# Attention with MoE on one core: order-only edges that put a unit's first steps on q behind a sum of the unit two before it

## Chip, core and metric

The kernel runs on one core of a Trainium2 chip. The metric is the device time of one execution in microseconds, the median of the runs. Engines: PE is TensorE, ACT ScalarE, DVE VectorE, POOL GpSimd; SP issues the DMAs.

## The reference

Attention with a causal mask and a memory term for 4 batches, 8 heads, 576 tokens and 64 features a head; its output, 2304 tokens by 512, goes through a two-matrix MLP with a squared ReLU.

```python
def _attn_ref(q, k, v, M_prev, z_prev, beta):
    scores = scale * np.matmul(q, k.transpose(0, 1, 3, 2))
    scores = np.where(causal, -1000000000.0, scores)
    a = np.exp(scores - scores.max(-1, keepdims=True))
    a /= a.sum(-1, keepdims=True) + 1e-09
    local = np.matmul(a, v)
    q_p = np.where(q > 0, q, np.exp(q) - 1.0) + 1.0
    mem_ret = np.einsum('bhsd,bhde->bhse', q_p, M_prev)
    mem_norm = np.einsum('bhsd,bhd->bhs', q_p, z_prev)[..., None] + 1e-06
    g = 1.0 / (1.0 + np.exp(-beta))[None, :, None, None]
    return g * (mem_ret / mem_norm) + (1 - g) * local

def _moe_ref(x, w_in, w_out):
    r = np.maximum(x @ w_in, 0.0)
    return (r * r) @ w_out
```

## The kernel before

The work is cut into 24 **units**. A unit is one batch, one pair of heads, and a list of query tiles of 128 tokens. Batches 0 and 1 (`SEG` is 2) have eight units each: the four head pairs with tiles 1 and 2, and then the four with tiles 3 and 4. Units 0 to 7 are batch 0, 8 to 15 batch 1. Batches 2 and 3 have four units each, with all four tiles (16 to 23). The first 64 tokens of every batch are handled ahead by `first_tokens`.

`attention` is a generator that writes down one unit. Its fore part: a cast of q to `qh` (ACT, L465) and the remainder `ql` (L466), the same for k (L471, L472), then phi(q): `Exp` of q into `pe` (ACT, L482), a ReLU (L487) and L488, then a scale for v (L504 to L521) and the memory term, products `pm` with the memory matrix (PE, L541) and a division. Units 0 to 5 have no casts: they multiply in full float32. The fore part ends with `after()`, which writes down the loads of the next units (`kd`, `qm`, `vv`; q stands in `qm`).

Then the rows of the unit, tile by tile in the order 2, 1, 3, 4: scores on PE (L577) into the one tile `sp`; on DVE the masked scores `e` and their extreme `mx` (L598); on ACT the exponential with its row sums in `sm` (L618; four `sm` buffers); the split of `e` into two halves `a` (ACT L656, DVE L658); a DMA transpose to `aT` (SP, L662); products with v into `acc` (PE, L682); and the sums that add `acc` to the features `feat` (DVE, L685, one for each head). The fore part of unit i+1 is written ahead of the rows of unit i.

When four units have finished a pair of tiles of their batch, their tokens form a block for the MoE (`moe`): `token_halves` scales `feat` into halves `hl` and transposes them to `xT`, and then follow `up` products (PE, L966 to L968), ReLU, square and `gh` (ACT, L972 to L975), `gl` (DVE) and the products `oacc` (PE, L937 to L939). Blocks 1 to 6 run as such; the last two blocks together in `moe_last`. Block 1 is batch 0, tiles 1 and 2 (units 0 to 3), block 2 its tiles 3 and 4 (units 4 to 7). The weights are converted by ACT and DVE in the first 120 us.

What stands where in each engine's queue is decided by a list scheduler when the program is built: it follows the order of writing as priority, its own costs, and edges. An edge of the class `NoSync` (`AFTER`) binds this scheduler alone: no semaphore comes of it, so the chip doesn't wait for the named instruction. An engine runs its queue in order.

Of the kernel before, what the change touches and what calls it, by code (L numbers as in the profile page):

```python
# [14 lines left out]
AF = mybir.ActivationFunctionType  # L15
# [52 lines left out]
SEG = 2  # L68
# [15 lines left out]
AFTER = mybir.DependencyInfo(mybir.DependencyClass.NoSync, mybir.DependencyReason.DATA)  # L84
# [15 lines left out]
def fused_kernel(ctx: ExitStack, tc: tile.TileContext, t0_d, kk_d, qv_d, beta, w_in, w_out, out):  # L100
    nc = tc.nc
# [329 lines left out]
    def loads(i):  # L431
# [13 lines left out]
        nc.sync.dma_start(vv[:, :nv], qv_d[b, p, :, SQ + 2 * ZW : SQ + 2 * ZW + nv])  # L445
        return kd, qm, vv

    def attention(b, p, tiles, ld, after, early, sfull, full, ap, ap_early):
        q_eng, k_eng = (nc.gpsimd if c == 'p' else nc.vector for c in (EARLY if early else LATE))
        late = 0 if early else 1  # L450
        h0 = 2 * p
        tl = tiles[-1]
        kn, ncn = sum(QT[tl]), tl + 1
        qa, qb = QT[tiles[0]][0] - D, kn - D
        kd, qm, vv = ld
        q_raw = qm[:, 2 * ZW :]
# [5 lines left out]
        if not sfull:  # L462
            qh, ql = (ap.tile([P, SQ], F32R, tag=t, name=t) for t in ("qh", "ql"))
            kh, kl = (ap.tile([P, S], F32R, tag=t, name=t) for t in ("kh", "kl"))
            nc.scalar.copy(qh[:, qa:qb], q_raw[:, qa:qb])  # L465
            low = q_eng.tensor_tensor(  # L466
                out=ql[:, qa:qb], in0=q_raw[:, qa:qb], in1=qh[:, qa:qb].bitcast(F32), op=ALU.subtract
            )
            parts.append(low)
            yield  # L470
            nc.scalar.copy(kh[:, :kn], kd[:, :kn])  # L471
            low = k_eng.tensor_tensor(out=kl[:, :kn], in0=kd[:, :kn], in1=kh[:, :kn].bitcast(F32), op=ALU.subtract)  # L472
            parts.append(low)
            yield
            terms = [(qh, kh), (ql, kh), (qh, kl)]
        else:
            terms = [(q_raw, kd)]

        pe = ap.tile([P, 2, S], F32, tag="e", name="pe", bufs=EB if ap is at else EB2)[:, 0]
        w = slice(qa, qb)  # L480
        lead = (b, p, tiles) == order[0]
        ex = nc.scalar.activation(pe[:, w], q_raw[:, w], AF.Exp)  # L482
        if lead:
            later("s", ex)
        ph = pe if sfull else q_raw
# [123 lines left out]
        for i in [t for t in TORD if t in tiles]:  # L609
# [6 lines left out]
            for h in range(2):  # L616
                bs = mx[:n, h, ns - 1 : ns]
                ex = nc.scalar.activation(  # L618
                    e[:n, h, :ke], e[:n, h, :ke], AF.Exp, bias=bs, scale=-1.0, accum_out=sm[:n, h : h + 1]
                )  # L620
# [61 lines left out]
                    nc.tensor.matmul(acc[:n, h], lhs[:, :n], rhs, start=x == 0, stop=x == len(mms) - 1)  # L682
            for h in range(2):
                xo = memx[:n, i - 1, h]
                nc.vector.scalar_tensor_tensor(  # L685
                    out=xo, in0=acc[:n, h], scalar=sm[:n, h : h + 1], in1=xo, op0=ALU.mult, op1=ALU.add
                )
            yield

    def runs(xs):  # L690
# [338 lines left out]
    order = []  # L1029
# [8 lines left out]
    def unit(i):  # L1038
        ld = nxt.pop(0)

        def after():
            while i + len(nxt) + 1 < min(len(order), i + (3 if i + 2 >= AHEAD else 2)):
                nxt.append(loads(i + len(nxt) + 1))

        ap = more[-1] if i > FIRST and i % 2 else at
        early = i < NEF and max(order[i][2]) < 4
        return attention(*order[i], ld, after, i < NEARLY, i < NES, early, ap, i >= WA)
# [87 lines left out]
```

## Time and profile before

| | us |
|---|---|
| three runs: median (lowest to highest) | 585.41 (581.78 to 586.48) |
| the profiled execution, its own time | 584.56 |
| its span, first to last instruction | 582.8 |
| PE, DVE, ACT busy | 527.8, 452.9, 413.1 |

The span is what the rows of the profile cover; the time of an execution has 1.8 us around it. Busy time of PE is that of its matmuls, whose ends are modelled and which overlap: how dense they are is read from their starts.

### The profile page before, as it was taken

Reading aid. Unit: us, or ns where it says so; the run is one execution under the profiler, and the core shown is the slowest. Engines: PE = TensorE matmul, PEld = TensorE weight load, DVE = VectorE, ACT = ScalarE, POOL = GpSimd, SP = SyncE. Lnnn points to the kernel's source line nnn. Section 1 sums busy time; section 2 is a strip of 40 time slices with the busy share of each in tenths; the row PEclk is TensorE's granted clock in tenths of the full one; section 3 lists DMA queues with packets and bytes.
Section 4 is the critical chain, followed back from the end, with each engine's and each line's share of the span. In section 5 each row is a group of like instructions: output and inputs, shape, how many; then the busy total and the mean of one; then the engine's idle time right before and its main releaser. Section 6 shows DMA issues by size and latency. Waiting matters only on the chain.

```text
span 582.8 us, 12609 instructions
## 1 busy us (share of the span) xinstructions
PE 527.8 (91%) x4767; PEld 370.4 (64%) x4767; DVE 452.9 (78%) x1421; ACT 413.1 (71%) x884; POOL 14.9 (3%) x20
## 2 busy tenths in 40 slices
PE   4668988989899988898999999999999999999997
PEld 3546765646576666566777767656677666447766
DVE  6898779798987767989888868696777587744745
ACT  3797997796877776977977768788677643557352
POOL 1010000100110000000000000000000000000000
PEclk9767987999899999999999989999999999999999
DMA  8943971578586556688485394626734440000002
GB/s 317 405 122 74 363 267 37 107 166 179 118 172 127 143 116 124 141 172 178 133 159 138 79 169 87 105 51 132 110 58 86 89 61 2 37 0 2 1 1 72
DMA packets 133132, 71.37 MB, mean 122 GB/s; under 512 B 115408, under 2 KB 121552, under 8 KB 133072
## 3 DMA queue, kind: packets, MB, share of 16 engines
q1 hardware_dynamic: 133072, 70.57, 52.2%
q8 instruction: 37, 0.61, 0.4%
q14 instruction: 23, 0.19, 0.1%
HBM read 37.53 MB, written 4.72 MB: 72 GB/s over the span
## 4 chain that ended last, share of the span: by engine, by line
PE 34%; DVE 31%; ACT 15%; DMA 13%; issue 5%; SPq 1%; POOL 0%; ACTq 0%; DVEq 0%
DVE e L598 5%; DVE a L658 5%; PE seven L834 4%; ACT e L618 4%; DMA aT<-a 3%; DMA qm<-in_qv_dram 3%; PE oacc L939 3%; PE oacc L937 3%; PE oacc L938 3%; PE up L967 3%; PE up L966 3%; PE up L968 3%; PE acc L682 3%; DMA raw<-in_w_in_dram 3%; PE seven L807 2%
## 5 line engine op out<-in xcount | busy, mean ns | idle before, releaser
L966 PE MATMUL up<-xT,w 128*128 128x256 f16 x448 | 123.3, 275 | 0.1
L967 PE MATMUL up<-xT,w 128*128 128x256 f16 x448 | 123.3, 275 | 0.0
L968 PE MATMUL up<-xT,w 128*128 128x256 f16 x448 | 123.2, 275 | 0.0
L618 ACT ACTIVATE e<-e,mx 128x320 f32<-128x320 f32 (+3 forms) x128 | 77.7, 608 | 40.5 <-DVE feat L685 31.4
L937 PE MATMUL oacc<-w,gh 128*128 128x512 f16 x224 | 86.5, 386 | 6.3 <-ACT gh L975 6.1
L938 PE MATMUL oacc<-w,gh 128*128 128x512 f16 x224 | 86.0, 384 | 0.0
L939 PE MATMUL oacc<-w,gl 128*128 128x512 f16 x224 | 82.0, 383 | 0.5 <-DVE gl L978 0.5
L658 DVE SCALAR_TENSOR_TENSOR a<-e,a 128x128 f16<-128x128 f32 x116 | 64.5, 566 | 18.6 <-ACT a L656 18.2
L656 ACT ACTIVATE a<-e 128x128 f16<-128x128 f32 x116 | 55.2, 523 | 8.7 <-DMA aT<-a 8.2
L967 PEld LDWEIGHTS <-w 128*128 128x128 f16 x448 | 44.2, 99 | 12.6 <-issue 1.8
L966 PEld LDWEIGHTS <-w 128*128 128x128 f16 x448 | 44.5, 99 | 10.8
L968 PEld LDWEIGHTS <-w 128*128 128x128 f16 x448 | 44.3, 99 | 8.0 <-issue 0.4
L682 PE MATMUL acc<-vs,aT 128*128 128x64 f16 x1138 | 42.0, 195 | 7.4 <-DMA aT<-a 4.9
L682 PEld LDWEIGHTS <-aT 128*128 128x128 f16 x1138 | 38.9, 99 | 13.7 <-DMA aT<-a 7.1
L598 DVE CUSTOM_DVE_ANT_0 e<-sp,mask 128x320 f32<-128x320 f32 (+3 forms) x128 | 47.2, 417 | 0.0
L972 ACT ACTIVATE r<-up,gam 128x512 f32<-128x512 f32 x48 | 32.4, 674 | 15.5 <-PE up L968 12.8
L978 DVE TENSOR_TENSOR gl<-r,gh 128x512 f16<-128x512 f32 x56 | 38.3, 684 | 6.1 <-ACT gh L975 5.2
L937 PEld LDWEIGHTS <-gh 128*128 128x128 f16 x224 | 22.2, 99 | 28.3 <-ACT gh L975 8.5
L939 PEld LDWEIGHTS <-gl 128*128 128x128 f16 x224 | 21.6, 98 | 25.0 <-issue 2.7
L685 DVE SCALAR_TENSOR_TENSOR feat<-acc,sm,feat 128x64 f32<-128x64 f32 x128 | 29.1, 276 | 9.1 <-PE acc L682 9.0
L834 PEld LDWEIGHTS <-g 128*128 128x128 f16 x336 | 32.7, 98 | 5.4 <-DVE g L760 1.2
L973 ACT ACTIVATE r<-r 128x512 f32<-128x512 f32 x56 | 35.0, 624 | 0.8
(192 smaller groups left out, 1033.1 us busy)
## 6 DMA issues: line engine op xcount, KB each, us to landing
raw<-in_w_in_dram SPq DMA_DIRECT2D x16, 512.0 KB, 7.7
raw<-in_w_out_dram SPq DMA_DIRECT2D x16, 512.0 KB, 8.3
vv<-in_qv_dram SPq DMA_DIRECT2D x16, 320.0 KB, 3.4
kd<-in_kk_dram SPq DMA_DIRECT2D x16, 288.0 KB, 3.1
out_dram<-o SPq DMA_DIRECT2D x12, 256.0 KB, 2.4
qm<-in_qv_dram SPq DMA_DIRECT2D x8, 321.0 KB, 3.1
qm<-in_qv_dram SPq DMA_DIRECT2D x8, 193.0 KB, 3.6
vv<-in_qv_dram SPq DMA_DIRECT2D x8, 192.0 KB, 4.5
```

The source lines that it names most:

```text
L598: nc.vector.tensor_tensor_reduce(out=e[:, h, ka:kb], in0=sps[:, h, cs], in1=mask[:, 448 - q0 + ka : 448 - q0 + kb], scale=-0.125, scalar=3 ...
L618: ex = nc.scalar.activation(e[:n, h, :ke], e[:n, h, :ke], AF.Exp, bias=bs, scale=-1.0, accum_out=sm[:n, h : h + 1])
L656: nc.scalar.mul(av[:, :, o0 : o0 + w], x, SC)
L658: nc.vector.scalar_tensor_tensor(out=av[:, :, o0 + w : o0 + 2 * w], in0=x, scalar=SC, in1=av[:, :, o0 : o0 + w], op0=ALU.mult, op1=ALU.sub ...
L682: nc.tensor.matmul(acc[:n, h], lhs[:, :n], rhs, start=x == 0, stop=x == len(mms) - 1)
L834: mms.append(nc.tensor.matmul(x[:, blk], g[j][:, i0, a, blk, p], t_side(j, p, m, i1), start=j == js[0] and p == n == 0, stop=j == js[-1] a ...
L937: nc.tensor.matmul(acc[t], gh[:, u, ts], w_out_op(f, 0), start=f == f0, stop=False)
L938: nc.tensor.matmul(acc[t], gh[:, u, ts], w_out_op(f, 1), start=False, stop=False)
L939: nc.tensor.matmul(acc[t], gl[:, u, ts], w_out_op(f, 0), start=False, stop=f == f1)
L966: nc.tensor.matmul(uo, w_in_op(f, k, 0), x_op(k, 0), start=k == 0, stop=False)
L967: nc.tensor.matmul(uo, w_in_op(f, k, 0), x_op(k, 1), start=False, stop=False)
L968: nc.tensor.matmul(uo, w_in_op(f, k, 1), x_op(k, 0), start=False, stop=k == NK - 1)
```

## The change

A dictionary `step` keeps, for each unit, its first `feat` sum. In batches 0 and 1 (`b < SEG`) a unit i has an order-only edge from that of unit i-2 to its cast `qh` and one to its `Exp` of q. Units 0 and 1 have none, and units 2 to 5, which have no cast, have the second alone. No instruction is added.

```diff
+    step = {}
+
+    def behind_unit(b, i, x):
+
+        if i in step and b < SEG:
+            tc.add_manual_dep(x.ins, step[i].ins.name, AFTER, reason="loads come late")
+        return x
+
     def attention(b, p, tiles, ld, after, early, sfull, full, ap, ap_early):
...
+        me = order.index((b, p, tiles))
...
-            nc.scalar.copy(qh[:, qa:qb], q_raw[:, qa:qb])
+            behind_unit(b, me - 2, nc.scalar.copy(qh[:, qa:qb], q_raw[:, qa:qb]))
...
-        ex = nc.scalar.activation(pe[:, w], q_raw[:, w], AF.Exp)
+        ex = behind_unit(b, me - 2, nc.scalar.activation(pe[:, w], q_raw[:, w], AF.Exp))
...
-                nc.vector.scalar_tensor_tensor(
+                x = nc.vector.scalar_tensor_tensor(
                     out=xo, in0=acc[:n, h], scalar=sm[:n, h : h + 1], in1=xo, op0=ALU.mult, op1=ALU.add
                 )
+                step.setdefault(me, x)
```

In the changed kernel the lines behind the first insertion have numbers 9 or 10 higher.

The first place is ACT's queue around the cast of unit 8 (`qh_2048`). `e_1951` and `a_1963` are tile 3 of unit 6, `e_2107` and `a_2159` tile 4 of unit 7, `qm_1789` is q of unit 7, and `r` belongs to MoE. Before:

```order
L618 ACTIVATE e_1951,sm_1953<-e_1951,mx_1952 128x448 x2
L487 ACTIVATE qm_1789<-qm_1789 128x256
L972 ACTIVATE r_5226<-up_5201,gam_78 128x512
L656 ACTIVATE a_1963<-e_1951 128x2x64
L656 ACTIVATE a_1963<-e_1951 128x2x384
L471 CAST kh_2050<-kd_1794 128x320
L465 CAST qh_2048<-qm_1796 128x256
```

And now:

```order
L480 CAST kh_2220<-kd_1932 128x320
L627 ACTIVATE e_2107,sm_2109<-e_2107,mx_2108 128x576
L474 CAST qh_2048<-qm_1796 128x256
L491 ACTIVATE pe_2056<-qm_1796 128x256
L627 ACTIVATE e_2107,sm_2109<-e_2107,mx_2108 128x576
L982 ACTIVATE r_5360<-up_5335,gam_78 128x512
L496 ACTIVATE qm_1796<-qm_1796 128x256
L665 ACTIVATE a_2159<-e_2107 128x2x64
```

The cast of unit 8 has moved behind tile 4 of unit 6 and tile 3 of unit 7, between the two exponentials of unit 7's tile 4; the cast of k (`kh`) of the next unit, 9, now stands ahead of it, and unit 8's `Exp` follows it at once.

The second place is PE's queue around the scores of unit 10 (`qh_2333`, written to `sp_2490`). `acc_2292` and `aT_2284` belong to unit 8, `pm_2245` to unit 9. Before:

```order
L541 MATMUL pm_2245<-qm_1934 128x130
L577 MATMUL sp_2490<-kh_2335,qh_2333 128x320 x2
L577 MATMUL sp_2490<-kh_2335,ql_2334 128x320 x2
L577 MATMUL sp_2490<-kl_2336,qh_2333 128x320 x2
L577 MATMUL sp_2490<-kh_2335,qh_2333 128x192 x2
L577 MATMUL sp_2490<-kh_2335,ql_2334 128x192 x2
L577 MATMUL sp_2490<-kl_2336,qh_2333 128x192 x2
L541 MATMUL pm_2245<-qm_1934 128x130
L682 LDWEIGHTS aT_2284
L682 MATMUL acc_2292<-vs_2071,aT_2284 128x64
```

And now (`w30_1347` is of block 1's last products, `xT_2199` the tokens of block 2):

```order
L948 MATMUL oacc_5234<-w30_1347,gh_5493 128x512
L586 MATMUL sp_2490<-kh_2335,qh_2333 128x320 x2
L586 MATMUL sp_2490<-kh_2335,ql_2334 128x320 x2
L586 MATMUL sp_2490<-kl_2336,qh_2333 128x320 x2
L586 MATMUL sp_2490<-kh_2335,qh_2333 128x192 x2
L586 MATMUL sp_2490<-kh_2335,ql_2334 128x192 x2
L586 MATMUL sp_2490<-kl_2336,qh_2333 128x192 x2
L976 LDWEIGHTS w0_465
L976 MATMUL up_5529<-xT_2199,w0_465 128x256
```

The scores of unit 10 stood right ahead of unit 8's first products `acc`; now they stand behind them, at the end of block 1, and the first `up` products of block 2 follow.

## Rows read from the trace of the kernel before

**Rows 1.** The page, part 1: busy us, share of the span, instructions

```profile
PE 527.8 (91%) x4767; PEld 370.4 (64%) x4767; DVE 452.9 (78%) x1421; ACT 413.1 (71%) x884; POOL 14.9 (3%) x20
```

**Rows 2.** Busy time by stretch: length; PE, PEld, DVE, ACT, POOL busy; clock, DMA, GB/s

```profile
0.00:100.00 100.00, 73.22 (x669) 55.32 (x670) 82.06 (x254) 80.88 (x180) 5.91 (x12) 0.81 0.67 231
100.00:280.00 180.00, 162.69 (x1582) 115.23 (x1581) 153.58 (x557) 137.59 (x316) 9.00 (x8) 0.99 0.70 146
280.00:460.00 180.00, 173.76 (x1728) 122.32 (x1725) 138.36 (x493) 134.75 (x310) 0.00 (x0) 0.99 0.56 104
```

**Rows 3.** Timeline of PE: start, us, engine, line, what; unit 8's scores at 160.60

```profile
160.07 0.27 PE L966 MATMUL up<-xT,w 128*128 128x256 f16 x1
160.18 0.27 PE L967 MATMUL up<-xT,w 128*128 128x256 f16 x1
...
160.60 0.41 PE L577 MATMUL sp<-kh,qh 64*128 64x320 f32 x2
...
161.55 0.64 PE L682 MATMUL acc<-vs,aT 128*128 128x64 f16 x16
...
191.14 0.38 PE L938 MATMUL oacc<-w,gh 128*128 128x512 f16 x1
191.36 0.38 PE L939 MATMUL oacc<-w,gl 128*128 128x512 f16 x1
```

**Rows 4.** Waits of PE from 100 to 280: in all, times, longest

```profile
PE oacc L937 <- ACT gh L975: 5.9, 6, 2.0
PE sp L577 <- DVE mx L598: 3.8, 2, 2.4
```

**Rows 5.** Waits of ACT from 100 to 280: in all, times, longest

```profile
ACT e L618 <- DVE feat L685: 11.0, 7, 2.2
ACT qh L465 <- DMA qm<-in_qv_dram: 9.4, 6, 2.9
...
ACT pe L482 <- DMA qm<-in_qv_dram: 3.2, 2, 1.9
```

**Rows 6.** Timeline of ACT; in brackets the idle time ahead and its releaser

```profile
164.85 0.41 ACT L465 CAST qh<-qm 128x256 fp32r<-128x256 f32 x1 [2.78 <-DMA qm<-in_qv_dram]
...
167.69 0.55 ACT L618 ACTIVATE e<-e,mx 128x320 f32<-128x320 f32 x1
...
211.19 0.67 ACT L618 ACTIVATE e<-e,mx 128x448 f32<-128x448 f32 x1 [1.36 <-DVE feat L685]
...
214.49 0.42 ACT L482 ACTIVATE pe<-qm 128x256 f32<-128x256 f32 x1 [1.31 <-DMA qm<-in_qv_dram]
214.81 1.03 ACT L656 ACTIVATE a<-e 128x128 f16<-128x128 f32 x2
```

**Rows 7.** Timeline of DVE: first `mx` of unit 8, `ql`, sums of units 6 and 7

```profile
163.94 0.48 DVE L598 CUSTOM_DVE_ANT_0 e<-sp,mask 128x320 f32<-128x320 f32 x1
...
165.32 0.41 DVE L466 TENSOR_TENSOR ql<-qm,qh 128x256 fp32r<-128x256 f32 x1
165.65 0.46 DVE L685 SCALAR_TENSOR_TENSOR feat<-acc,sm,feat 128x64 f32<-128x64 f32 x2
...
180.25 0.47 DVE L685 SCALAR_TENSOR_TENSOR feat<-acc,sm,feat 128x64 f32<-128x64 f32 x2
```

**Rows 8.** Timeline of SP's queue: transposes of unit 8, of block 2, of unit 12

```profile
170.65 2.81 SPq L662 DMA_TRANSPOSE aT<-a  x2
...
186.21 2.77 SPq L717 DMA_TRANSPOSE xT<-hl  x2
...
216.92 1.54 SPq L662 DMA_TRANSPOSE aT<-a  x1
```

**Rows 9.** DMA issues: queue, kind, times, median us to landing

```profile
aT<-a SPq DMA_TRANSPOSE x58, 4.1
...
xT<-hl SPq DMA_TRANSPOSE x16, 3.4
```

**Rows 10.** Busy time by stretch as in rows 2, a stretch behind attention

```profile
500.00:520.00 20.00, 20.00 (x94) 9.11 (x93) 11.19 (x17) 10.57 (x12) 0.00 (x0) 1.00 0.07 27
```

## The prediction

> **What bounds the kernel now.** I read the page's first part, then the busy times by stretch. TensorE (PE) is busy 91% of the span, VectorE (DVE) 78%, ScalarE (ACT) 71% [rows 1]. PE's idle time by stretch [rows 2]: 26.8 us in the first 100, 17.3 in 100 to 280 (180 less 162.69), 6.2 in 280 to 460, and the tail behind attention is nearly gapless. The clock is granted at 0.99 from 100 us on [rows 2], which is its upper level, 2.4 GHz.
>
> Is a busy PE at its peak? Consecutive `up` products start 0.11 us apart and the 512-wide products 0.22 us apart, also in the middle of attention [rows 3]. So between 100 and 460 us PE does little but stream, and MoE products of earlier tokens fill it while attention waits on other engines. The work on PE is the same in both kernels, so **the time changes by what is added to or taken from PE's idle time**, and the first edge falls at unit 2, near 47 us. What is at stake above all is the 17.3 us of 100 to 280, where units 4 to 15 run.
>
> The same window by waits: PE waits 5.9 us in six places for `gh` (ACT is late) and 3.8 us in two for `mx` (DVE is late) [rows 4]. ACT waits 9.4 us for `qm` ahead of the cast to `qh`, 3.2 us ahead of `Exp` on q, and 11.0 us at the softmax's exponential, marked as behind a `feat` sum [rows 5]. The last one is the ring of four `sm` buffers: a unit's first exponential needs the buffer that unit i-2's first sum has read. A single case shows the harm: at 214.49 ACT had waited 1.31 us for q of unit 14, and the split `a` of unit 12 stood behind it, at 214.81 [rows 6].
>
> **The change, part by part.** No instruction is added or removed and no semaphore: the edges bind the order alone. (1) *Cast and Exp on q go back in ACT's queue.* In the first piece of the order, unit 8's cast stood behind the first split of unit 6 and now stands behind two tiles more. Its load has long landed there: loads of q are released by the `pm` products, which already come about with unit i-2's sums. So the `qm` waits of units 5 to 15 go, at most 9.4 + 3.2 = 12.6 us of ACT's time, 30% of its 42.4 us idle (180 less 137.59) [rows 2]. ACT is not what PE is short of, so only PE's waits on late ACT and DVE work count, 5.9 + 3.8 = 9.7 us [rows 4]. I take 30% of them, **3 us gained**; bounds 0 (others are last then) and 9.7.
>
> (2) *The scores follow the cast.* In the trace unit 8's scores start at 160.60 [rows 3], 5.05 us ahead of unit 6's sum at 165.65 [rows 7]; with the edge they come behind the cast and the subtraction (0.41 us each [rows 6, 7]). That was not the unit's limit: its exponential stood for the `sm` buffer till 167.69 [rows 6]. But what was done early was cover. I counted PE's work between a unit's first score and its first sum product, in the two orders, at the spacings of [rows 3]. Before, units 8 to 15 have 20.2, 21.4, 20.7, 23.3, 25.1, 23.3, 19.9 and 23.6 us. Now they have 15.7, 13.4, 10.6, 13.7, 12.1, 14.2, 11.3 and 17.9. (Unit 10 now: 54 `up` at 0.11 is 5.9, 8 wide products at 0.22 is 1.8, two units' scores at 0.95 is 1.9, 26 sum products at 0.04 is 1.0; 10.6.)
>
> What must fit there: scores 1.0, four `mx` steps 1.4 (163.94 to 165.32) [rows 7], exponential to transpose 3.0 (167.69 to 170.65) [rows 6, 8], landing 4.1 [rows 9]; 9.5 us where nothing queues. With the queues of unit 8 it is 160.60 to 170.65 plus 4.1, 14.2 us. Units 12 to 15, with tiles 3 and 4, need 2.7 more (211.19 to 216.92 is 5.7 against 3.0) [rows 6, 8]. PE's clock time is longer than its work by 180 / 162.69, so the covers stretch by 1.106. At the low need nothing is short. At the high need and without stretch the eight units lack 18.0 us. At the middle (12 and 14.6, stretched) units 10, 12 and 14 lack 0.3, 1.2 and 2.1: 3.6, **4 us lost**. I take the middle because ACT's queue loses the waits of (1) but DVE's keeps its length.
>
> (3) *Blocks of MoE that wait for attention.* Block 2 needs unit 7's last sum. From it (180.25) [rows 7] to the second transpose's landing (186.21 + 1.4 + 3.4 [rows 8, 9], 191.0) takes 10.8 us; PE's work between that unit's last product and the block's first falls from 13.3 to 11.3 us. Block 1's cover falls from 14.5 to 11.9, but on ACT the cast of unit 6's k and a split of unit 5 no longer stand ahead of its halves. I take 0, bound 2.6 for the two.
>
> (4) *Queues.* On SP the loads and transposes change places by one or two; the transposes of block 1 now stand ahead of unit 5's and of a load. On DVE the subtraction and unit 8's features move with the cast; GpSimd keeps its twelve steps in their order. Batches 2 and 3 carry no edge; attention's last product stands behind 365.0 us of PE work instead of 361.9, so the tail is 3.1 shorter: no change in the sum.
>
> **Sum.** 584.56 us (this execution: span 582.8 and 1.8 around it) - 3 + 4 + 0 = 585.6. The execution is 0.85 under the median of the three runs, 585.41, so against medians the forecast is **586.4**, 0.2% above. The three runs lie 4.7 us apart, and I take 1% (579.6 to 591.3) as what can be told from no change. The forecast's own range, from half the gain to twice the loss and the other way round, is 580 to 591.
>
> **Rivals.** *The waits were the brake (faster).* PE's waits for `gh` and `mx` go whole, and the covers hold at the low need: 584.56 - 9.7 = 574.9; with 2 us of it lost at the covers, 577. For it: rows like that at 214.49, where a wait for q holds a split that was ready. Against: ACT's largest wait, 11.0 us, stays, as the buffer ring is unchanged.
>
> *The cover is too thin (slower).* One mechanism: sum products stand in PE's queue with 10.6 to 14.2 us of work behind the scores, and their transposes have not landed; PE stops, and all MoE work behind them with it. At the high need 584.56 + 18.0 - 3 = 599.6, and at two thirds of the shortage 593.6. It decides from a need of about 13 us for tiles 2 and 1, and 15.5 for tiles 3 and 4. For it: unit 8 took 14.2. Against: units 8 to 15 now have fewer things in flight at once.
>
> *Attention, not PE, sets the pace (slower by more).* In a stretch with no PE gap at all, 500 to 520, weight loads are busy 9.11 of 20 us [rows 10], so 64% in 100 to 280 (115.23 of 180 [rows 2]) is no sign of room; the starts 0.11 apart are. If PE had room all the same, the loop from sum to sum would set the time. The sum to the exponential takes 2.0 us now (165.65 to 167.69) and then cast, subtraction, scores and `mx`, 3.2 us, or 6.5 with the 3.3 that unit 8's scores stood for DVE. Five loops in each of two strands at 1.2 to 4.5 more give 6 to 23: 591 to 608. The Trainium skill (Perfetto Trace Analysis, section Identifying the Most-Contended Engine) says that matmul busy time is no good measure and that busy LDWEIGHTS time is one; by it PE has a third of its time free, and this rival holds. The trace speaks against that, as the gapless stretch shows.
>
> *Nothing moves.* Excluded by the order.
>
> **How the numbers follow.** Forecast 0.47, thin cover 0.25, waits were the brake 0.25, pace 0.03. The orders of batches 2 and 3 are dealt anew as well, and 6.2 us of idle time there can turn either way. Eight in ten reach from 575 (the faster rival's end) to 600 (the high need). Faster by over 1%: 0.25; within: 0.47; slower: 0.28.
>
> **What would show it.** Right: no ACT wait for `qm` ahead of `qh` in units 6 to 15; PE idle in 100 to 280 near 18; some of its waits now for `aT` or its landing at the sum products. Wrong, fast: PE idle there under 12 with the `gh` rows gone. Wrong, slow: over 25, with sum products waiting for `aT`, or MoE `up` products standing for `xT`. Wrong in kind: if idle time before 100 us, where weights are converted, moves by more than 5 us, or if that of batches 2 and 3 does.

## The result and the profile after

The changed kernel takes **564.82 us** (median of four runs, 562.50 to 565.98) against 585.53 for the kernel before, run beside it: ratio 0.9653, 95% interval 0.9601 to 0.9705. The forecast was 586.4 with a range of 575 to 600; it missed, and the range too. The profiled execution took 562.5 us, its span is 560.7, 22.1 shorter than before.

The page's first part of the changed kernel, in the columns of [rows 1]:

```profile
PE 519.1 (93%) x4767; PEld 367.1 (65%) x4767; DVE 453.0 (81%) x1421; ACT 410.7 (73%) x884; POOL 16.6 (3%) x20
```

The 22.1 us are 13.4 of PE's idle time (55.0 to 41.6) and 8.7 of its busy time, with the same number of products. Busy time by stretch, as [rows 2]:

```profile
0.00:100.00 100.00, 74.34 (x706) 56.57 (x707) 83.63 (x258) 82.56 (x187) 8.01 (x13) 0.86 0.64 231
100.00:280.00 180.00, 174.41 (x1707) 124.21 (x1705) 166.10 (x602) 148.30 (x338) 8.57 (x8) 1.00 0.72 157
280.00:460.00 180.00, 174.19 (x1717) 123.80 (x1716) 141.05 (x478) 131.87 (x297) 0.00 (x0) 1.00 0.54 102
```

PE's idle time in 100 to 280 fell from 17.3 to 5.6 us: 11.7 of the 13.4. Ahead of 100 it fell by 1.1, in 280 to 460 by 0.4, and the tail has 4.6 in both. DVE and ACT do 12.5 and 10.7 us more work in those 180 us than before, and PE starts 1707 products there instead of 1582: more of the program falls into the same stretch.

PE's waits from 100 to 280 in the kernel before, in the columns of [rows 4], from the third row on. The first two are those of [rows 4], 5.9 and 3.8 us:

```profile
PE vt L508 <- DVE feat L552: 2.6, 3, 1.6
PE vt L508 <- DVE feat L685: 2.0, 2, 1.2
PE acc L682 <- DVE feat L552: 1.9, 2, 1.8
PE acc L682 <- DVE feat L685: 0.5, 1, 0.5
```

Here `vt` (the scale of v) and `acc` wait for DVE's steps on `feat`; what else there is comes to 0.4 us, half of it for `aT`. In the changed kernel these rows are gone, and those of `gh` and `mx` are the last two:

```profile
PE acc L691 <- DMA aT<-a: 1.9, 4, 0.8
...
PE up L976 <- DMA xT<-hl: 0.3, 1, 0.3
PE oacc L947 <- ACT gh L985: 0.3, 1, 0.3
PE sp L586 <- DVE mx L607: 0.3, 1, 0.3
```

And ACT's in the same stretch, the whole of what is over 1.5 us:

```profile
ACT e L627 <- DVE mx L607: 16.6, 11, 3.1
ACT vs L528 <- DVE vy L522: 2.9, 3, 1.5
ACT r L982 <- PE up L978: 2.0, 1, 2.0
```

All three rows of [rows 5] are gone: the waits for q (9.4 + 3.2 us), which the edges are about, and the 11.0 us of the exponential at unit i-2's sums, which the prediction held to stay. In their place ACT waits 16.6 us for `mx`, so DVE is now what ACT waits for. That costs PE little, as its own idle time shows. The place of [rows 6] in the new timeline of ACT (exponential of unit 12, cast and `Exp` of the next unit's q, split of unit 12):

```profile
206.60 0.67 ACT L627 ACTIVATE e<-e,mx 128x448 f32<-128x448 f32 x1 [2.74 <-DVE mx L607]
...
207.92 0.39 ACT L474 CAST qh<-qm 128x256 fp32r<-128x256 f32 x1
208.21 0.41 ACT L491 ACTIVATE pe<-qm 128x256 f32<-128x256 f32 x1
208.53 1.03 ACT L665 ACTIVATE a<-e 128x128 f16<-128x128 f32 x2
```

Before, the split came 3.62 us after its exponential (211.19 to 214.81), 1.31 of it ACT's wait for another unit's q; now 1.93 after it, with no wait between.

A second place, which the prediction passed over, is ACT's queue near 100 us. The kernel before:

```profile
97.55 0.62 ACT L656 ACTIVATE a<-e 128x128 f16<-128x128 f32 x2
102.26 0.42 ACT L482 ACTIVATE pe<-qm 128x256 f32<-128x256 f32 x1 [4.09 <-DVE a L658]
102.58 0.72 ACT L638 COPY aF<-pxa 64x128 f32<-64x128 f32 x4
...
110.40 1.04 ACT L656 ACTIVATE a<-e 128x128 f16<-128x128 f32 x2 [3.96 <-DMA aT<-a]
```

The changed kernel:

```profile
96.71 0.89 ACT L647 COPY aF<-pxa 64x128 f32<-64x128 f32 x4 [0.65 <-PE pxa L642]
...
98.38 0.41 ACT L491 ACTIVATE pe<-qm 128x256 f32<-128x256 f32 x1
```

Before, `Exp` of unit 4's q stood 4.09 us for its buffer of the ring `e`, and the copies `aF` of unit 2, whose sum comes next, stood behind it. (`pe` takes its buffer from the same ring as the scores' `e`.) The edge turned the two round, and the wait of 3.96 us some 8 us later is 0.87 in the changed kernel.

### The profile page after: what moved, and what is told of

Same layout as the page of the kernel before. It is cut to its first block, busy times and chain, and to the rows that moved or that the text cites. A ratio compares the mean times of both kernels' runs of the same rounds, so it can differ in the third digit from the quotient of the medians.

```text
span 560.7 us, 12604 instructions
## 1 busy us (share of the span) xinstructions
PE 519.1 (93%) x4767; PEld 367.1 (65%) x4767; DVE 453.0 (81%) x1421; ACT 410.7 (73%) x884; POOL 16.6 (3%) x20
## 4 chain that ended last, share of the span: by engine, by line
PE 36%; DVE 29%; ACT 19%; DMA 11%; issue 3%; SPq 0%; POOL 0%; ACTq 0%; DVEq 0%
DVE e L607 5%; DVE a L667 5%; ACT e L627 5%; DMA aT<-a 4%; PE seven L844 4%; PE oacc L949 3%; PE up L976 3%; PE oacc L948 3%; PE oacc L947 3%; PE up L978 3%; PE up L977 3%; ACT a L665 3%; PE seven L815 2%; PE seven L817 2%; PE seven L816 2%
## 5 line engine op out<-in xcount | busy, mean ns | idle before, releaser
L947 PE MATMUL oacc<-w,gh 128*128 128x512 f16 x224 | 84.8, 379 | 3.4 <-ACT gh L985 3.3
L948 PE MATMUL oacc<-w,gh 128*128 128x512 f16 x224 | 84.9, 379 | 0.0
L667 DVE SCALAR_TENSOR_TENSOR a<-e,a 128x128 f16<-128x128 f32 x116 | 64.6, 566 | 12.3 <-ACT a L665 11.7
L947 PEld LDWEIGHTS <-gh 128*128 128x128 f16 x224 | 21.9, 98 | 23.6 <-ACT gh L985 4.5
L948 PEld LDWEIGHTS <-gh 128*128 128x128 f16 x224 | 21.9, 98 | 19.8
```

What stands on the lines that cost most here:

```text
L667: nc.vector.scalar_tensor_tensor(out=av[:, :, o0 + w : o0 + 2 * w], in0=x, scalar=SC, in1=av[:, :, o0 : o0 + w], op0=ALU.mult, op1=ALU.sub ...
L947: nc.tensor.matmul(acc[t], gh[:, u, ts], w_out_op(f, 0), start=f == f0, stop=False)
L948: nc.tensor.matmul(acc[t], gh[:, u, ts], w_out_op(f, 1), start=False, stop=False)
```

## The experiments

The theories, as their expectations name them. **Queue theory**: what cost time was ACT standing, in order, at a step of a younger unit that could not yet be done, with older units' work behind it; the time goes where these waits go, however they are removed. Its *sum-wait* form (formed after the first four runs) puts the weight on the exponential's wait for unit i-2's sum, its *cast* form on the casts' waits for q. **Early-work theory**: the waits don't matter; the early casts, subtractions, scores and minima push older work aside. **Reshuffle theory**: any edge makes the scheduler deal the whole order anew, and the gain is luck of the deal. **Cover theory**: the prediction's second term, later starts leave PE short of cover.

The first four runs cut the edges in two, by units and by step, and give q one more buffer.

**Edges on units 2 to 5 alone.**

```diff
-        if i in step and b < SEG:
+        if i in step and i + 2 < 6:
```

> The edges on units 2 to 5 alone; these units make no cast of q, so that only their Exp comes behind unit i-2's first sum. Queue theory (the time came from ScalarE's queue, where it stood at a step on q that could not yet be done while older units' work stood behind): the changed kernel gained some 6 us of TensorE's standing ahead of block 1, where these units run, and the rest later, so this kernel gains about 6: 579 us (576 to 582), and ScalarE's waits of casts on qm, about 9 us in 40:265, stay. Reshuffle theory (any edge deals the whole order anew and the gain hangs on the deal, not on the waits): no tie between the place of the edges and the place of the gain; anything from 565 to 595. Early-work theory (what a cast, a subtraction and a score done too early push aside on ScalarE and VectorE is what costs): units 2 to 5 have hardly any such work ahead of their scores, so 583 to 586.

577.50 us, ratio 0.9863 (0.9820 to 0.9907): 7.8 gained. Both waits near 100 us are gone, those for q and for sums are not.

**Edges on units 6 to 15 alone.**

```diff
-        if i in step and b < SEG:
+        if i in step and 6 <= i + 2 and b < SEG:
```

> The edges on units 6 to 15 alone, the other half. Queue theory: the early stretch stays as before (block 1 starts near 128, Exp of unit 4 waits 4 us), the waits of casts on qm go, and 13 to 17 us come from the stretches of blocks 1 to 3: 571 us (567 to 575). Together with the run of units 2 to 5 the gains add up to 20.7. Reshuffle theory: the two halves do not add up. Early-work theory: nearly the whole gain, 565 to 570.

570.18 us, 0.9750 (0.9714 to 0.9786): 15.1 gained. The waits for q and sums are gone, those near 100 us (3.3 and 4.2) stay. The halves make 22.9, the whole change 20.7: they add up, within the intervals, which the reshuffle theory did not expect.

**Three buffers of q, no edges** (the kernel before).

```diff
-        qm = lp.tile([P, 2 * ZW + SQ], F32, tag=f"qm{n}", name="qm")
+        m = i % 3
+        qm = at.tile([P, 2 * ZW + SQ], F32, tag=f"qm{m}", name="qm")
```

> The kernel before, without any edge, with three buffers of qm in turn instead of two, so that the load of q does not wait for unit i-2's last reader. Casts stay early in ScalarE's order. Queue theory: ScalarE no longer waits for qm (12.6 us before, 1 to 5 after) and what those waits held up comes earlier: 571 to 579 us. Early-work theory: the early casts, subtractions and scores are still there, so no gain: 582 to 588. Reshuffle theory: no forecast of sign; 570 to 600.

574.70 us, 0.9831 (0.9792 to 0.9869). The time is in the queue theory's span, its condition is not: ACT still waits 8.4 us for q. With earlier loads the scheduler set the first casts earlier still: unit 6's comes at 94.0 instead of 129.1.

**Edges on `Exp` alone.**

```diff
-            behind_unit(b, me - 2, nc.scalar.copy(qh[:, qa:qb], q_raw[:, qa:qb]))
+            nc.scalar.copy(qh[:, qa:qb], q_raw[:, qa:qb])
```

> Edges on Exp alone, none on the cast of qh. Queue theory: units 2 to 5 are as in the changed kernel (6 us), the casts of units 6 to 15 may stand at qm again (some 9 us on ScalarE): 574 to 580 us. Early-work theory: casts, subtractions and scores come early again, Exp alone late: 578 to 584. Reshuffle theory: anywhere from 565 to 595.

570.43 us, 0.9764 (0.9722 to 0.9805), better than the queue and the early-work theory said; the wide span of the reshuffle theory holds it. The casts' waits for q stay (6.9 us), but the sum waits are gone. That gave the sum-wait form, which the next runs tested.

**Six buffers of `sm`, no edges.**

```diff
-                        at.tile([P, 2], F32, tag="sm", name="sm", bufs=4),
+                        at.tile([P, 2], F32, tag="sm", name="sm", bufs=6),
```

> The kernel before, without edges, with six buffers of the sums of Exp (sm) instead of four, so that Exp of unit i's scores does not wait for the sums of unit i-2. Sum-wait theory (formed on the first four runs: the late half of the gain came and went with ScalarE's waits of Exp of the scores for unit i-2's sum, 11.0, 11.5 and 11.9 us in before and in the two runs that gained 0 to 11, none in those that gained 15 and more): these waits go and 8 to 15 us with them, 570 to 578 us. Cast theory (the waits of casts on q cost): those stay, 583 to 587. Early-work theory: the early work stays, 583 to 590.

576.93 us, 0.9888 (0.9854 to 0.9923). Sum waits fell from 11.0 to 5.2 us and waits for q rose from 12.6 to 18.7: ACT stands as long as before, at another place. In time it is the sum-wait form's, barely, and its gain of 6.5 us is under the 8 to 15 forecast; as a test of one wait it failed. The two waits near 100 us are still there (3.25 and 4.53 us):

```profile
101.74 0.42 ACT L482 ACTIVATE pe<-qm 128x256 f32<-128x256 f32 x1 [3.25 <-DVE a L658]
...
110.45 1.04 ACT L656 ACTIVATE a<-e 128x128 f16<-128x128 f32 x2 [4.53 <-DMA aT<-a]
```

**Edges on the cast alone.**

```diff
-        ex = behind_unit(b, me - 2, nc.scalar.activation(pe[:, w], q_raw[:, w], AF.Exp))
+        ex = nc.scalar.activation(pe[:, w], q_raw[:, w], AF.Exp)
```

> Edges on the cast of qh alone, none on Exp of q. Units 2 to 5, which have no such cast, are as before. Sum-wait theory: with the cast behind unit i-2's first sum the scores and their Exp come later too, Exp no longer waits for the sum, and the late half of the gain is there: 568 to 574 us. If it was the place of Exp of q itself that counted (its buffer of the ring e is taken early), 580 to 586.

569.71 us, 0.9760 (0.9728 to 0.9793), as the sum-wait form said. Near 100 us the waits are nearly as before, since units 2 to 5 have no cast. Either edge takes the sum waits away. In time the one on the cast does most of the late half (13.7 of 15.1 us); the one on `Exp` makes 14.9 with units 2 to 5 in it, where the two halves make 22.9.

**Edges from unit i-3.** Both `me - 2` become `me - 3`.

> The same edges, from unit i-3's first sum instead of unit i-2's: a looser tie, which most steps meet anyway. Sum-wait theory and cast theory: most waits stay, 579 to 587 us. Reshuffle theory: an edge anywhere gives a new order and a time that has nothing to do with its tightness, 565 to 595.

571.54 us, 0.9798 (0.9762 to 0.9835). The looser edge was not met already: it took waits for q down to 2.5 and for sums to 7.0. The queue theory's number was wrong because its guess at the waits was. The reshuffle theory's span, 565 to 595, holds the time here too.

**Three buffers of q and six of `sm`, no edges.** Both of the edits above, on the kernel before.

> The kernel before without edges, with three buffers of qm and six of sm: both kinds of wait go, the early work stays early. Queue theory in any form (waits in ScalarE's queue are what costs): 563 to 573 us. Early-work theory: 580 to 590.

567.80 us, 0.9724 (0.9688 to 0.9760): 15.6 gained with no edge at all. The waits for q are 5.0 and for sums 7.4 us, together half of what they were. The casts are not late here: the cast of unit 12 (the seventh in ACT's queue) stands at 190.74 and the first sum of unit 10 at 205.77.

```profile
190.74 0.41 ACT L466 CAST qh<-qm 128x256 fp32r<-128x256 f32 x1
```
```profile
205.77 0.48 DVE L686 SCALAR_TENSOR_TENSOR feat<-acc,sm,feat 128x64 f32<-128x64 f32 x2
```

The early-work theory falls with this run, which it put at 580 to 590, and with the one on `Exp` alone.

**A buffer of its own for unit 4's `Exp`, no edges.**

```diff
-        pe = ap.tile([P, 2, S], F32, tag="e", name="pe", bufs=EB if ap is at else EB2)[:, 0]
+        if order.index((b, p, tiles)) == 4:
+            pe = at.tile([P, SQ], F32, tag="pe4", name="pe", bufs=1)
+        else:
+            pe = ap.tile([P, 2, S], F32, tag="e", name="pe", bufs=EB if ap is at else EB2)[:, 0]
```

> The kernel before, without edges, with a buffer of its own for Exp of q of unit 4, which in before stood 4.1 us at the ring e in ScalarE's queue. Queue theory: by the line through the ten kernels so far (about 0.5 us of time for each us that ScalarE stands at q, at unit i-2's sums, at the ring e and at the buffer of a unit's transposed weights) the 4.1 us alone give 2, and with the 4.0 us wait that follows it 4: 581 to 584 us; if this stretch counts in full, as the run with the edges on units 2 to 5 had it, 577 to 579. Reshuffle theory: anything from 570 to 595.

576.97 us, 0.9890 (0.9841 to 0.9938). The 4.1 us wait is gone, the one behind it fell from 4.0 to 1.4, and 6.7 us are gained, as by the edges on units 2 to 5. The later waits grew (q 16.5, sums 15.4), so the gain is not theirs. It is what the queue theory gave if that stretch counts in full; the reshuffle theory's span holds it as well.

**Edges from unit i-1.** Both `me - 2` become `me - 1`.

> The changed kernel with edges from unit i-1's first sum instead of unit i-2's: every unit's first steps wait for the unit just ahead. Queue theory: ScalarE has no wait left to lose, so no gain; what is new is the cost of starting late. Cover theory (the second term of the prediction): units' work between scores and products falls further, TensorE waits for minima, transposes and products: 570 to 590 us. If cover costs nothing even now: 562 to 568.

583.94 us, 1.0015 (0.9985 to 1.0044). It is not the kernel that its expectation tells of: the fore part of unit i is written ahead of the rows of unit i-1, so `step` has no entry yet and no edge is made, but for `Exp` of units 1 and 4. What ran is a control: two edges, an order dealt anew on every engine but GpSimd, and the waits still there.

```profile
ACT e L627 <- DVE feat L694: 12.1, 11, 2.0
ACT qh L474 <- DMA qm<-in_qv_dram: 7.3, 5, 2.7
```

With 20.6 us of the waits left it takes the time of before: this one new deal gave nothing. But unit 4's `Exp`, one of the two steps with an edge, no longer stands for its buffer, and the wait behind it is gone too; ACT stands at an `up` product of MoE instead:

```profile
106.50 0.60 ACT L982 ACTIVATE r<-up 128x512 f32<-128x512 f32 x1 [4.16 <-PE up L978]
...
107.66 0.40 ACT L491 ACTIVATE pe<-qm 128x256 f32<-128x256 f32 x1
```

So a kernel without the two waits near 100 us gained nothing, and the one with six `sm` gained 6.5 with both.

**The changed kernel with both buffers.** The two buffer edits, on the changed kernel.

> The changed kernel with three buffers of qm and six of sm as well. Edges have taken those waits in batches 0 and 1 already, so the buffers have nothing to take there. Queue theory: 562 to 567 us, the changed kernel's time, though the order is dealt anew; in batches 2 and 3 ScalarE stood 25 us at sums with TensorE 3 of 60 us idle, so little comes there. Reshuffle theory: a scatter like that between the other kernels, 560 to 580.

559.62 us, 0.9578 (0.9548 to 0.9608), 5 better than the changed kernel and under both spans, the second by 0.4 us: the buffers did have something to take.

**Edges in all batches.**

```diff
-        if i in step and b < SEG:
+        if i in step:
```

> The same edges in all four batches. In batches 2 and 3 of the changed kernel TensorE was idle 5.8 of 180 us, although ScalarE stood 25 us at unit i-2's sums there. Queue theory with TensorE's work as cover: at most 3 us to gain, 562 to 567. If ScalarE's waits cost 0.5 us each us wherever they are: 550 to 555. If the later starts thin the cover of the last units: 566 to 575.

569.04 us, 0.9752 (0.9720 to 0.9783), 4 worse than the changed kernel, in the span of the third case. PE is idle 7.5 us instead of 5.6 in 100 to 280 and 7.3 instead of 5.8 in 280 to 460, where its waits for `aT` are 6.4 us instead of 4.1; of PE's work 102.1 us are left behind 460 instead of 96.1. Whether the edges there did it is not shown: the kernel with edges from the last sum, below, loses as much without them.

**Edges on units 2 to 5 and both buffers.** The first edit and the two buffer edits, on the changed kernel.

> The edges on units 2 to 5 alone, with three buffers of qm and six of sm: each wait is taken away where it stands, and casts, scores and minima of units 6 to 15 stay as early as in the kernel before. Queue theory: the gains of the run with these edges (7.8) and of the run with both buffers (15.6, some of it in the same early stretch) come together: 559 to 565 us, as the changed kernel with both buffers (559.6). Early-work theory: the late starts of units 6 to 15 are missing, 566 to 575.

576.43 us, 0.9898 (0.9865 to 0.9931). The waits are not off: the scheduler set the first casts earlier again (unit 6's at 92.5), and ACT's waits are all there.

```profile
ACT qh L475 <- DMA qm<-in_qv_dram: 14.3, 8, 3.7
ACT e L628 <- DVE feat L695: 9.1, 7, 2.8
ACT pe L492 <- DMA qm<-in_qv_dram: 5.0, 3, 2.5
```

So it doesn't test early work, as it was meant to; it is one more kernel with the waits, and has the time of such a kernel. The early-work span ends at 575, and the queue theory's, which added the gains of 7.8 and 15.6, at 565: gains don't add where each edit gives the scheduler another order.

**Edges from unit i-2's last sum.**

```diff
-                step.setdefault(me, x)
+                step[me] = x
```

> The changed kernel with the edges from unit i-2's last sum instead of its first, 2 to 8 us later by the times of the changed kernel: no wait of ScalarE is left to take, and the cover between scores and products falls by that much more. Cover theory (the second term of the prediction, 1 us for some 9 us of cover in the changed kernel): from some point TensorE waits for minima, transposed weights and products, 567 to 580 us. If cover still costs nothing: 562 to 567.

570.24 us, 0.9792 (0.9746 to 0.9839), 5 worse than the changed kernel. That is in the cover theory's span, but not where it looks. In 100 to 280 PE is idle 6.5 us against 5.6. Its loss is in 280 to 460, where no unit of batches 2 and 3 has an edge: 10.1 against 5.8, with waits for `aT` of 7.6 us instead of 4.1:

```profile
PE acc L691 <- DMA aT<-a: 7.6, 6, 1.8
```

**The changed kernel with six `sm` buffers alone.** The edit of `sm`, on the changed kernel.

> The changed kernel with six buffers of sm alone, to tell which of the two buffers gave the 5 us that the run with both gained over it. By the waits left in the changed kernel (25 us of ScalarE at unit i-2's sums in batches 2 and 3, none at qm before 265): it is sm, 558 to 562 us. If it is qm: 563 to 567.

559.65 us, 0.9610 (0.9582 to 0.9639): by its time six `sm` alone give the 5 us that both buffers gave, as expected. By its ratio they give about half of that, and the intervals of the two kernels overlap, so a small share of the third buffer of q can't be excluded. PE's idle time in 280 to 460 is 0.9 us instead of 5.8. These two kernels are the fastest here.

**All together**, from the waits and busy times of 100 to 280 (ACT's waits are those of cast and `Exp` for q, and of the exponential for sums):

| kernel | us | for q | for sums | PE idle |
|---|---|---|---|---|
| before | 585.5 | 12.6 | 11.0 | 17.3 |
| edges i-1 (two) | 583.9 | 8.5 | 12.1 | 11.0 |
| units 2 to 5 | 577.5 | 10.5 | 13.5 | 12.4 |
| own buffer, unit 4 | 577.0 | 16.5 | 15.4 | 13.0 |
| six `sm` | 576.9 | 18.7 | 5.2 | 13.0 |
| units 2 to 5, both buffers | 576.4 | 19.3 | 9.1 | 11.7 |
| three `qm` | 574.7 | 8.4 | 12.6 | 11.0 |
| edges i-3 | 571.5 | 2.5 | 7.0 | 7.2 |
| `Exp` alone | 570.4 | 6.9 | 0.2 | 7.4 |
| last sum | 570.2 | 0 | 0 | 6.5 |
| units 6 to 15 | 570.2 | 0 | 0 | 5.6 |
| cast alone | 569.7 | 1.5 | 0 | 5.8 |
| all batches | 569.0 | 0 | 0 | 7.5 |
| both buffers, no edges | 567.8 | 5.0 | 7.4 | 10.4 |
| changed | 564.8 | 0 | 0 | 5.6 |
| changed, six `sm` | 559.7 | 0 | 0 | 4.9 |
| changed, both buffers | 559.6 | 0 | 0 | 4.8 |

Where the two waits sum to 20 us or more, PE is idle 11.0 to 17.3 us and the kernel takes 574.7 to 585.5; where they sum to at most 12.4, it is idle 4.8 to 10.4 and takes 559.6 to 571.5. No kernel crosses over, though the line is drawn after the fact, and the ratios of the two kernels next to it (three `qm`, edges i-3) have intervals that overlap. The kernel before, run beside each set of experiments, took 582.5 to 585.5 us, so 2 or 3 us between two rows tell nothing. The reshuffle theory, that the gain has nothing to do with the waits, falls by the table as a whole and by the halves that add up; most of the times by themselves lay in its wide spans. What is left of it is the spread inside a group, 11 to 12 us, which the two waits don't order: the own buffer has the longest waits of all, 31.9 us, and is 6.7 faster than the kernel before, which has 23.6.

## Why the prediction was wrong

**The frame held, as far as can be told.** It said that the time changes by PE's idle time: between the two profiled executions 13.4 of 22.1 us did. The other 8.7 are PE's busy time. The mean granted clock was 0.961 in one and 0.976 in the other, and busy time times clock is 507 in both (527.8 x 0.961, 519.1 x 0.976; 504 to 512 across the other kernels), so the 8.7 fit a clock that fell less often. That the change did that is not shown: the clock differs as much between executions of one kernel. The 34 executions of the kernel before that ran beside the experiments had 0.960 to 0.979. The eight at 0.964 or less took 584.6 us in the median and the five at 0.974 or more 582.5, so such a difference of clock went with 2 us, not 8.7. An estimate from the same product: the execution of the kernel before at 0.977 (584.26 us, span 582.5) was busy some 519 us and idle 63.5 (give or take 4, as the product spreads), against 41.6 in the changed kernel at 0.976. So at a like clock most of the gain may be PE's idle time.

**Step (1) failed: the price of ACT's waits.** "ACT is not what PE is short of, so only PE's waits on late ACT and DVE work count", 9.7 us, of which 3 were taken. PE's idle time in 100 to 280 fell by 11.7, beyond the bound. The 9.7 are two rows only, those of `gh` and `mx`. The waits of `vt` and `acc` for DVE's steps on `feat`, 7.0 us in the same view, are late DVE work as well and were left out; they went too. With them and a row of 0.2, late ACT and DVE work makes 16.9 of PE's 17.3 us idle, of which the rows that name ACT are 5.9. So a chain that begins at a waiting ACT can reach PE under DVE's name; that it did so here is argued from the rows that went together, not followed link by link.

**A reason against the fast rival was false.** "ACT's largest wait, 11.0 us, stays, as the buffer ring is unchanged." The ring is unchanged and the wait went: with the cast or `Exp` behind unit i-2's first sum, the exponential comes later still, when that sum is done. The runs with either edge alone show it (0 and 0.2 us of sum waits). The rival itself, "the waits were the brake", was right in kind, and the sign that it gave (PE idle under 12 with the `gh` rows gone) came. Its 575 to 577 were 10 to 12 us too high, since it was priced by the same 9.7 us, and at 0.25 it was too unlikely. The sign "wrong in kind" did not come: PE's idle time moved by 1.1 us ahead of 100 and by 0.4 in 280 to 460.

**Step (2), 4 us lost, was overpriced.** The scores did start later, and PE's waits for `aT` in 100 to 280 rose from 0.2 to 1.9 us, half of the 3.6 counted. With the still later edges PE is idle 0.9 us more there: the cover was thin on paper and held. The need was counted with queues as they stood before; that a unit's own chain runs faster once ACT does not stand is likely, but no run shows it by itself. The slow rival falls with it for batches 0 and 1.

**Step (3) was right**: PE's wait of `up` for `xT` is 0.3 us. **The sum** adds up, but its range of 580 to 591 starts from the profiled execution, where the forecast of 586.4 starts from the median; by the median it is 581 to 592.

**Step (4) passed over units 2 to 5**, which have an edge on `Exp`: it names batches 2 and 3 and closes with "no change in the sum". The rows were there to be read: an `Exp` 4.09 us at its buffer with older copies behind it. What that is worth is open. Two kernels that take the 8.1 us near 100 away or shorten them gained 7.8 and 6.7 us, one of them without an edge; but the two-edge control has neither wait and gained nothing, and six `sm` gained 6.5 with both. Where the gain lands is unclear as well: with the own buffer PE's idle time ahead of 100 fell by 1.5 us, in 100 to 280 by 4.3.

**The pace rival** (attention, not PE, sets the time) falls: starts are later and the time is less. PE is now idle 5.6 us of 180, while weight loads are busy 124.21. The Trainium skill (Perfetto Trace Analysis, section Identifying the Most-Contended Engine), which the prediction weighed there, has busy LDWEIGHTS time, together with MFU (the share of peak FLOPs that the matmuls do), as the measure of PE's headroom. By the weight loads alone nearly a third of PE's time would be free; the trace again shows no such room.

**Open.** How much of the 20.7 us the waits explain. The changed kernel lies 10 to 13 us under the five kernels that keep the waits and are faster than `before`. Those five lie 8 to 11 us under `before`, though their waits are little or no shorter, and the two-edge control does not. For that part, and for the 4 us of PE's idle time that the last-sum edges add in batches that have none, the new deal of the order is all that the rows offer. The waits could not be removed by buffers with the order held, since the scheduler dealt the order anew with each buffer and, with a third buffer of q, set the first casts earlier.

## What to carry to other kernels

In an engine that runs its queue in order, a step that waits costs what stands behind it: read the row right after a wait, and when that row belongs to older work that was ready, put the step behind it, by an order-only edge or a buffer. Bound what such a wait can cost by all the idle time of the bounding engine in that stretch, here 17.3 us, not by the rows that carry the waiting engine's name, 5.9; and don't take a wait further down the same queue for fixed: it moves with the step. Where a scheduler deals the order, every edit is also a new deal: kernels with much the same waits lay 8 us and more apart here, so one run of one edit does not tell its cause.

## What was not expected of the hardware

The granted clock fell in one execution and not in another after like idleness. By 5 us, from 80 on, the profiled execution of the kernel before:

```profile
80.00:85.00 5.00, 2.88 (x34) 2.18 (x32) 5.00 (x10) 5.00 (x9) 0.00 (x0) 0.85 0.57 187
85.00:90.00 5.00, 4.61 (x18) 2.69 (x17) 4.14 (x26) 5.00 (x14) 0.00 (x0) 0.50 0.34 103
```

and that of the changed kernel:

```profile
80.00:85.00 5.00, 2.30 (x29) 1.57 (x27) 5.00 (x13) 5.00 (x10) 0.00 (x0) 1.00 0.62 197
85.00:90.00 5.00, 3.20 (x20) 1.82 (x21) 4.48 (x24) 4.93 (x10) 0.00 (x0) 1.00 0.19 53
```

In the first, PE was busy 2.88 of 5 us and then ran at 0.50, the lower level of 1.2 GHz. In the second it was busy less (2.30, then 3.20) and stayed at 2.4 GHz. These are one execution each, so they don't show that the change moved the clock. No sum over waits shows a fall of the clock, and PE's busy time of two single executions can differ by it.
